# Converting the weights of the second MLP's first five chunks beside the first MLP, by way of HBM

## The chip, the cores and the metric

The kernel runs on one core of one Trainium2 chip. The metric is the device time of one execution in microseconds (us); the times of several runs are given by their median. The engines are TensorE (PE, with its weight loads as PEld), VectorE (DVE), ScalarE (ACT), GpSimd (POOL) and SyncE (SP), which here issues every transfer.

## What is computed

Three stages follow one another. A memory attention gives x, 2304 tokens by 512. The first MLP (d_ff 2048) and the second, bilinear one (d_ff 1536) follow:

```
a = softmax(phi, over the sequence);  k_m = a^T k;  v_m = a^T v
x = softmax(q k_m^T / 8) v_m                  # 4 batches, 8 heads, 576 tokens
h = x @ w_in;  g = max(0.01 h, h);  y = g @ w_out
out = ((y @ w_a) * (y @ w_b)) @ w_out2
```

All weights reach the kernel as 64-bit floating point numbers, seen as pairs of 32-bit words.

## The kernel before

**Weights.** Every weight tile (512 KB, 128 partitions x 512 numbers) is loaded by one transfer and converted on the chip by `weight()`. ACT takes the high and the low word apart (lines 441, 444), then come a clamp (448, DVE or POOL), a shift (452, DVE), a join (456, DVE) and an addition (459, DVE or POOL), which leave a 32-bit number. That number is split into two parts of the matmul's type: a high part (a copy, line 366 on ACT or 368 on DVE) and a low part (a subtraction, 465 for w_in and w_out, 957 for the matrices of the second MLP; DVE or POOL). Each product of two matrices takes three passes: high by high, high by low, low by high.

**First MLP.** It runs over four chunks of 512 hidden columns and, in each, over eight blocks of 288 tokens: four h units (line 759) and four y units (789) per block. The first layer is not applied to x: `vw` first multiplies v_m by the chunk's w_in (line 710), and h is that by the attention weights. The y parts are added up over the chunks in the tiles acc (DVE, line 801; the first chunk by a copy).

**Second MLP.** It runs in two sweeps over halves of the tokens, and in each over twelve chunks of 128 hidden columns. A chunk's two products are built from seven products (`ab_unit`, line 1001; tiles abx, aby, abz) of sums of the weight blocks (`w_sums`, line 940) with sums of the blocks of y (`y_blocks`, lines 836 and 866: tiles yt and yb). The tokens that are left over, 64 of each batch, go through in the first sweep directly (`y_left`, `left_unit`, 1044). The output product (`o_unit`, 1070) comes every second chunk, and its results are added up on DVE (1083). In the first sweep a chunk loads wa, wb and w_out2, converts and sums them, and `keep_weights` stores the five finished tiles (four wo, one w_out2) in HBM; in the second sweep `w_back` reads them from there.

**Order.** The program first lists all operations with the engines on which each can run, its estimated cost, the tokens that it reads and writes, and its tiles. A planner (`Program.order`) then plays the program through with these costs and writes down one order for each engine. PE's main units have written positions; every other operation has a due time that follows from the units that need it. An operation starts in the plan when its inputs are ready, its due time is no further off than `ahead`, and, if it opens a tile, more than `keep` rooms are free (24 "slot" rooms, and 20 "big" rooms that slots may use as well). Among those that are ready the one that is due first goes first. The plan lets only one of DVE and POOL work on SBUF operands of this kind at a time (`Port`). On the chip each engine then goes through its list in order and waits for its inputs; this holds for SP's transfers too.

Of the kernel before, what the change touches and what calls it, by code (L numbers as in the profile page):

```python
# [45 lines left out]
}  # L46


LEAD = 12
SLACK = {'win0': 5.57, 'wout0': 7.97, 'win': 4.58, 'wout': 5.1, 'wa': 2.19, 'wb': 5.78, 'wout2': 1.6, ('sc', 0, 0): 5.86, ('sc', 0, 1): 1.95, ('sc', 1, 0): 4.58, ('sc', 1, 1): -2.11, ('sc', 2, 0): 6.27, ('sc', 2, 1): 9.76, ('vw', 0, 0): 11.17, ('vw', 0, 1): 11.03, ('vw', 0, 2): 6.36, ('vw', 1, 0): -4.57, ('vw', 1, 1): 5.86, ('vw', 1, 2): 14.74}  # L50
START = 25.0
# [26 lines left out]
def c_dma(nbytes):  # L78
    return max(0.6, nbytes / 355e3)
# [239 lines left out]
def tile_mem_attention__leaky_mlp__bilinear_mlp(  # L319
# [37 lines left out]
    def two(n):  # L357

        return Port({"DVE": c_dve(n), "POOL": c_pool2(n)})

    def copy_by(n, psum=False):
        return (dict if psum else Port)({"ACT": c_act(n), "DVE": (c_dve(n) if psum else c_dve2(n)) + BIAS})
# [58 lines left out]
        "wout2": lambda c, k: w_out2[c * FC2:(c + 1) * FC2, :],  # L421
    }

    def weight(kind, c, k):
        key, raw, cv = (kind, c, k), ("raw", kind, c, k), ("cv", kind, c, k)
        tile_of(raw, "slot", [512], I64)
        if kind not in ("wa", "wb"):
            tile_of(key, "slot", [2, 512], F32R, heir_of=raw)
        tile_of(cv, "slot", [2, 512], I32)
        late = kind in ("wa", "wb", "wout2")  # L430
        first = kind in ("win", "wout") and c == 0

        def load(T):
            src = src_of[kind](c, k)
            nc.sync.dma_start(T[raw] if len(src.shape) == 2 else T[raw].rearrange("p (j f) -> p j f", j=src.shape[1]), src)

        def words(T, t, w):
            return T[raw].bitcast(t).rearrange("p (n t) -> p n t", t=2)[:, :, w]

        def high(T):  # L440
            nc.scalar.activation(T[cv][:, 0, :].bitcast(F32), words(T, F32, 1), AF.Abs)

        def low(T):
            nc.scalar.activation(T[cv][:, 1, :], words(T, U32, 0), AF.Copy, scale=2.0 ** -29)

        def clamp(T, e):
            a = T[cv][:, 0, :].bitcast(F32)
            engines[e].tensor_scalar(a, a, W_LEAST, W_MOST, op0=ALU.max, op1=ALU.min)

        def shift(T):  # L450
            a = T[cv][:, 0, :]
            nc.vector.tensor_scalar(a, a, 3, 0x3FFFFFF8, op0=ALU.logical_shift_left, op1=ALU.bitwise_and)

        def join(T):
            a = T[cv][:, 0, :]
            nc.vector.scalar_tensor_tensor(a, words(T, I32, 1), -0x40000000, a, op0=ALU.bitwise_and, op1=ALU.bitwise_or)  # L456

        def add(T, e):
            engines[e].tensor_tensor(T[cv][:, 0, :], T[cv][:, 0, :], T[cv][:, 1, :], op=ALU.add)

        def hi(T, e):
            copy(e, T[key][:, 0, :], T[cv][:, 0, :].bitcast(F32))

        def lo(T, e):
            engines[e].tensor_tensor(T[key][:, 1, :], T[cv][:, 0, :].bitcast(F32), T[key][:, 0, :].bitcast(F32), op=ALU.subtract)

        a = ("a", key)
        op("DMA", c_dma(524288), load, w=[raw], tiles=[raw], ahead=30.0, keep=2 if late else 7 if c < 2 else 4)
        op("ACT", 0.66, high, r=[raw], w=[a], tiles=[raw, cv], ahead=25.0, keep=0 if late else 5 if c < 2 else 2)
        op("ACT", 0.66, low, r=[raw], w=[("l", key)], tiles=[raw, cv])  # L470
        op(Port({"DVE": 0.42, "POOL": 2.0}), 0, clamp, w=[a], tiles=[cv])
        op(Port({"DVE": 0.42}), 0, shift, w=[a], tiles=[cv])
        op(Port({"DVE": 0.68}), 0, join, r=[raw], w=[a], tiles=[raw, cv])
        op(Port({"DVE": 0.62, "POOL": 1.35}), 0, add, r=[("l", key)], w=[a], tiles=[cv])
        if kind in ("wa", "wb"):
            return
        op(copy_by(512), 0, hi, r=[a], w=[("hi", key)], tiles=[cv, key])
        op(two(512), 0, lo, r=[a, ("hi", key)], w=[key], tiles=[cv, key], slack=SLACK[kind + "0" if first else kind])


    def kv_part(b, g):
# [431 lines left out]
            places[k] = hbm.tile([P, 2, 512], F32, name="k_" + "_".join(map(str, k)))  # L913
        return places[k]

    def w_sums(c):

        cvs = {"A1": ("cv", "wa", c, 0), "A2": ("cv", "wb", c, 0)}
        done = {"A1": ("a", ("wa", c, 0)), "A2": ("a", ("wb", c, 0))}
        ws = ("ws", c)  # L920
        tile_of(ws, "slot", [4, 256])

        def val(T, name):
            if name[0] == "S":
                return T[ws][:, int(name[1]) - 1, :]
            i = int(name[2]) - 1
            return T[cvs[name[:2]]][:, 0, i * 256:(i + 1) * 256].bitcast(F32)

        def tok(name):
            return (ws, name) if name[0] == "S" else done[name[:2]]  # L930

        def of(name):
            return ws if name[0] == "S" else cvs[name[:2]]

        for name, x, y, alu in (
            ("S1", "A21", "A22", ALU.add), ("S2", "S1", "A11", ALU.subtract), ("S3", "A11", "A21", ALU.subtract), ("S4", "A12", "S2", ALU.subtract)
        ):
            op(
                two(256), 0,
                lambda T, e, name=name, x=x, y=y, alu=alu: engines[e].tensor_tensor(val(T, name), val(T, x), val(T, y), op=alu),  # L940
                r=[tok(x), tok(y)], w=[tok(name)], tiles=[ws, of(x), of(y)],
            )
        for i, names in enumerate((("A11", "A12"), ("A21", "A22"), ("S1", "S2"), ("S3", "S4"))):
            k = ("wo", 0, c, i)
            if i < 2:
                tile_of(k, "slot", [2, 2, 256], F32R, heir_of=("raw", ("wa", "wb")[i], c, 0))
            else:
                tile_of(k, "slot", [2, 2, 256], F32R)
            wide = (
                (lambda T, i=i: T[cvs[f"A{i + 1}"]][:, 0, :].bitcast(F32).rearrange("p (x f) -> p x f", x=2))  # L950
                if i < 2 else (lambda T, i=i: T[ws][:, 2 * i - 4:2 * i - 2, :])
            )
            r = list(dict.fromkeys(tok(x) for x in names))
            op(copy_by(512), 0, lambda T, e, k=k, wide=wide: copy(e, T[k][:, :, 0, :], wide(T)), r=r, w=[(k, 0)], tiles=[k, of(names[0])])
            op(
                two(512), 0,
                lambda T, e, k=k, wide=wide: engines[e].tensor_tensor(  # L957
                    T[k][:, :, 1, :], wide(T), T[k][:, :, 0, :].bitcast(F32), op=ALU.subtract
                ),
                r=[*r, (k, 0)], w=[k], tiles=[k, of(names[0])], slack=5.0,  # L960
            )

    def keep_weights(c):
        for k in [("wo", 0, c, i) for i in range(4)] + [("wout2", c, 0)]:
            op(
                "DMA", c_dma(524288),
                lambda T, k=k: nc.sync.dma_start(kept(k).rearrange("p a b -> p (a b)"), flat(T[k])),
                r=[k], w=[("kept", k)], tiles=[k], ahead=1e12,
            )
# [2 lines left out]
        t = t.rearrange("p a b c -> p (a b c)") if len(t.shape) == 4 else t.rearrange("p a b -> p (a b)")  # L972
        return t.bitcast(F32)

    def w_back(c):
        for k in [("wo", 0, c, i) for i in (0, 2, 3, 1)] + [("wout2", c, 0)]:
            back = ("wo", 1, c, k[3]) if k[0] == "wo" else ("wout2", c, 1)
            tile_of(back, "slot", [2, 2, 256] if k[0] == "wo" else [2, 512], F32R)
            op(
                "DMA", c_dma(524288),  # L980
                lambda T, k=k, back=back: nc.sync.dma_start(flat(T[back]), kept(k).rearrange("p a b -> p (a b)")),
                r=[("kept", k)], w=[back], tiles=[back], ahead=30.0, keep=2,
            )
# [122 lines left out]
    for c in range(NC1):  # L1106
        for k in range(4):
            weight("win", c, k)
        for bs in ([0], [1], [2, 3]) if c == 0 else ([0, 1], [2, 3]):
            vw(c, bs)  # L1110
        for k in range(4):
            weight("wout", c, k)
        for n in range(NBLK):
            for f in range(4):
                h_unit(c, n, f, (step, (-6, -5, -3, -1)[f]))
            for e in range(4):
                y_unit(c, n, e, (step + 1, (-4, -2, 0, 1)[e]))
            step += 1
    y_blocks(0)
    y_left()  # L1120
    y_blocks(1)
    queue = []
    for s in range(2):
        if s:
            y_back(1)
        for c in range(NC2):
            if s:
                w_back(c)
            else:
                weight("wa", c, 0)  # L1130
                weight("wb", c, 0)
                w_sums(c)
                weight("wout2", c, 0)
                keep_weights(c)
# [50 lines left out]
```

## Time and profile before

| | |
|---|---|
| median of 3 runs | 837.1 us (835.94 to 838.3) |
| profiled execution | 838.8 us, span 836.7 us |
| PE busy | 799.5 us (96%) |
| DVE busy | 643.9 us (77%) |
| ACT busy | 360.2 us (43%) |
| POOL busy | 247.6 us (30%) |
| mean granted clock of PE | 0.988 |
| moved by DMA | 135.32 MB |

The span reaches from the first to the last instruction of the profiled execution; its time lies 2.1 us above its span. The busy shares are means over stages that differ: attention and the start of the first MLP to about 140 us, the first MLP to about 405, the first sweep of the second to about 640, the second sweep after that.

### The profile page before, as it was taken

What the parts mean: (1) busy time and instruction counts of PE and PEld (TensorE: products, weight loads), DVE (VectorE), ACT (ScalarE), POOL (GpSimd) and SP (SyncE); (2) the same over time, 40 slices, a digit from 0 to 9 for tenths busy, and PEclk for the clock granted to TensorE, in tenths of its full rate; (3) what the DMA queues carried; (4) which work ended last, traced back from release to release, by engine and by line L of the source; (5) the groups of instructions that cost most, each with busy time, mean ns of one, the idle gap of its engine ahead of it and who ended that gap; (6) DMA issues with size and microseconds to landing.
All of it is one profiled execution on the core that took longest, in us unless ns stands there. A gap on an engine that the chain in (4) does not pass through costs nothing.

```text
span 836.7 us, 13050 instructions
## 1 busy us (share of the span) xinstructions
PE 799.5 (96%) x4922; PEld 709.3 (85%) x4922; DVE 643.9 (77%) x1133; ACT 360.2 (43%) x788; POOL 247.6 (30%) x228
## 2 busy tenths in 40 slices
PE   5889999999999999988879999999999999999997
PEld 4578998999999999988768888888888888888886
DVE  6998898469846985799999999989965444565655
ACT  5665886556445645455446544534411121110100
POOL 4462376012201310166776334535520000000000
PEclk9999999999999999999989999999999999999999
DMA  9894300320121001014775777665578878545302
GB/s 327 315 286 144 127 2 0 111 92 1 51 82 71 1 1 51 27 52 178 256 259 212 273 283 268 225 243 191 187 271 320 310 229 271 202 151 176 125 1 101
DMA packets 50606, 135.32 MB, mean 162 GB/s; under 512 B 6384, under 2 KB 19696, under 8 KB 50544
## 3 DMA queue, kind: packets, MB, share of 16 engines
q1 hardware_dynamic: 50544, 134.50, 46.1%
q8 instruction: 38, 0.62, 0.3%
q14 instruction: 24, 0.20, 0.1%
HBM read 90.96 MB, written 43.52 MB: 161 GB/s over the span
## 4 chain that ended last, share of the span: by engine, by line
PE 75%; DVE 15%; DMA 4%; issue 4%; ACT 1%; POOL 1%; SPq 0%; DVEq 0%; ACTq 0%
PE y L789 20%; PE o L1070 15%; PE h L759 10%; PE aby L1001 9%; PE abx L1001 6%; PE abz L1001 6%; PE vw L710 2%; PE a L1044 2%; DVE t L1009 1%; PE b L1044 1%; DMA kvr<-in_kv_rest_dram 1%; DVE g L775 1%; DVE cv_wout L456 1%; PE sc L627 1%; DVE wo L957 1%
## 5 line engine op out<-in xcount | busy, mean ns | idle before, releaser
L789 PE MATMUL y<-g,wout 128*128 128x288 f32 x1536 | 224.5, 299 | 9.8 <-DVE acc L801 7.8
L789 PEld LDWEIGHTS y<-g,wout 128*128 128x128 f32 x1536 | 212.6, 191 | 14.5 <-DVE acc L801 9.4
L1070 PE MATMUL o<-p,wout 128*128 128x512 f32 x576 | 142.3, 391 | 1.5 <-DVE p L743 0.8
L1070 PEld LDWEIGHTS o<-p,wout 128*128 128x128 f32 x576 | 107.9, 188 | 25.8 <-DVE p L743 1.1
L1001 PE MATMUL aby<-yb_T,wo 128*128 128x512 f32 x432 | 112.3, 396 | 6.2 <-DVE t L1009 6.2
L1001 PEld LDWEIGHTS aby<-yb_T,wo 128*128 128x128 f32 x432 | 80.6, 189 | 23.9 <-DVE t L1009 7.5
L736 ACT ACTIVATE g<-h 128x288 fp32r<-128x288 f32 x128 | 52.6, 411 | 89.9 <-PE h L759 87.2
L1009 DVE TENSOR_TENSOR t<-aby,t 128x512 f32<-128x512 f32 x72 | 49.4, 686 | 52.6 <-PE aby L1001 50.2
L1083 DVE TENSOR_TENSOR oacc<-o,oacc 128x512 f32<-128x512 f32 x80 | 55.0, 688 | 37.9 <-PE o L1070 37.6
L759 PE MATMUL h<-ahi,vwh 128*128 128x288 f32 x256 | 77.3, 302 | 1.2 <-ACT ahi L366 1.2
L775 DVE TENSOR_TENSOR g<-t,g 128x288 fp32r<-128x288 f32 x100 | 57.9, 586 | 26.7 <-ACT t L736 26.6
L759 PE MATMUL h<-alo,vwh 128*128 128x288 f32 x256 | 76.7, 300 | 0.5 <-POOL alo L658 0.5
L759 PE MATMUL h<-ahi,vwl 128*128 128x288 f32 x256 | 76.2, 298 | 0.0
L366 ACT CAST p<-t 128x512 fp32r<-128x512 f32 x44 | 27.2, 621 | 109.7 <-DVE t L1022 83.5
L1001 PE MATMUL abx<-yb_B,wo 128*128 128x512 f32 x288 | 73.7, 391 | 0.0
L775 POOL TENSOR_TENSOR g<-t,g 128x288 fp32r<-128x288 f32 x28 | 24.5, 882 | 131.5 <-ACT t L736 101.2
L1001 PEld LDWEIGHTS abx<-yb_B,wo 128*128 128x128 f32 x288 | 53.6, 189 | 10.8
L801 DVE TENSOR_TENSOR acc<-y,acc 128x288 f32<-128x288 f32 x96 | 43.3, 451 | 24.5 <-PE y L789 23.7
L736 ACT ACTIVATE t<-h 128x288 f32<-128x288 f32 x128 | 52.2, 408 | 0.0
L759 PEld LDWEIGHTS h<-ahi,vwh 128*128 128x128 f32 x256 | 48.9, 191 | 2.7 <-ACT ahi L366 1.4
L759 PEld LDWEIGHTS h<-alo,vwh 128*128 128x128 f32 x256 | 49.1, 192 | 0.9 <-POOL alo L658 0.9
L759 PEld LDWEIGHTS h<-ahi,vwl 128*128 128x128 f32 x256 | 49.1, 192 | 0.0
(173 smaller groups left out, 1360.4 us busy)
## 6 DMA issues: line engine op xcount, KB each, us to landing
k_wo<-wo SPq DMA_DIRECT2D x48, 512.0 KB, 6.6
wo<-k_wo SPq DMA_DIRECT2D x48, 512.0 KB, 4.7
raw_wout<-in_w_out_dram SPq DMA_DIRECT2D x28, 512.0 KB, 5.2
raw_win<-in_w_in_dram SPq DMA_DIRECT2D x16, 512.0 KB, 4.8
kv<-in_kv_dram SPq DMA_DIRECT2D x16, 512.0 KB, 7.8
raw_wa<-in_w_a_dram SPq DMA_DIRECT2D x12, 512.0 KB, 3.8
raw_wb<-in_w_b_dram SPq DMA_DIRECT2D x12, 512.0 KB, 4.6
k_wout<-wout SPq DMA_DIRECT2D x12, 512.0 KB, 5.2
```

The costliest lines, as they stand in the source:

```text
L366: nc.scalar.copy(dst, src)
L710: nc.tensor.matmul(T[o][0:m], T[VM[v]][:, j, bs[0]:bs[0] + len(bs), :].rearrange("p b m -> p (b m)"), T[w][:, i, wcols], start=(k == 0), s ...
L736: nc.scalar.activation(dst, src, AF.Prelu, alpha=0.01)
L759: nc.tensor.matmul(T[o], T[w[u]][:, k, fs], T[a[v]][:, k, cols], start=(k == 0 and i == 0), stop=(k == 1 and i == 2))
L775: lambda T, e: engines[e].tensor_tensor(T[g][:, i, 1, :], T[t], T[g][:, i, 0, :].bitcast(F32), op=ALU.subtract),
L789: nc.tensor.matmul(T[o], w[:, u, es], g[:, v, :], start=(f == 0 and i == 0), stop=(f == 3 and i == 2))
L801: "DVE", c_dve(NB), lambda T: nc.vector.tensor_tensor(T[acc][:, e, :], T[o], T[acc][:, e, :], op=ALU.add),
L1001: nc.tensor.matmul(T[o], T[w][:, which, u, k * P:(k + 1) * P], T[ys[v]][:, k, :], start=first and k == 0 and x == 0, stop=k == 1 and x == ...
L1009: op("DVE", 0.69, lambda T: nc.vector.tensor_tensor(T[to], T[o], T[x], op=ALU.add), r=[o, x], w=[to], tiles=[o, x, to])
L1044: nc.tensor.matmul(T[o], T[w][:, k // 2, u, k % 2 * P:(k % 2 + 1) * P], T[ys[v]][:, k, :], start=(k == 0 and x == 0), stop=(k == 3 and x = ...
L1070: nc.tensor.matmul(T[o], T[w][:, u, es], T[g][:, at, v, :], start=(x == 0 and k == 0), stop=(x == 1 and k == 2))
L1083: "DVE", c_dve(size), lambda T: nc.vector.tensor_tensor(T[acc][:, i, :], T[o], T[acc][:, i, :], op=ALU.add),
```

## The change

With `PRE = 5`, the operations that load, convert, sum and store the weights of chunks 0 to 4 of the second MLP are listed ahead of the y blocks, under version -1. Their loads read a token: for chunk 0 that the second chunk's last w_out tile of the first MLP is converted, for the others that the first wo tile of the chunk before is stored. They have no due time that holds them back (`ahead` is 1e12), but a load needs more than eight free rooms and the first ACT step more than six. In the first sweep, chunks 0 to 4 then read their five tiles back with `w_back`, as the second sweep does for all chunks; the second sweep reads the same stored tiles. Chunks 5 to 11 stay as they were. No operation computes anything else than before.

```diff
+PRE = 5
-    def weight(kind, c, k):
+    def weight(kind, c, k, after=()):
+        early = k < 0
...
-        op("DMA", c_dma(524288), load, w=[raw], tiles=[raw], ahead=30.0, keep=2 if late else 7 if c < 2 else 4)
-        op("ACT", 0.66, high, r=[raw], w=[a], tiles=[raw, cv], ahead=25.0, keep=0 if late else 5 if c < 2 else 2)
+        any_time = 1e12 if early else 60.0
+        op("DMA", c_dma(524288), load, r=after, w=[raw], tiles=[raw], ahead=1e12 if early else 30.0, keep=8 if early else 2 if late else 7 if c < 2 else 4)
+        op("ACT", 0.66, high, r=[raw], w=[a], tiles=[raw, cv], ahead=1e12 if early else 25.0, keep=6 if early else 0 if late else 5 if c < 2 else 2)
...
-    def w_sums(c):
+    def w_sums(c, v=0):
...
-    def keep_weights(c):
+    def keep_weights(c, v=0):
...
-    def w_back(c):
-        for k in [("wo", 0, c, i) for i in (0, 2, 3, 1)] + [("wout2", c, 0)]:
-            back = ("wo", 1, c, k[3]) if k[0] == "wo" else ("wout2", c, 1)
+    def w_back(c, s):
+        v = -1 if c < PRE else 0
+        for k in [("wo", v, c, i) for i in (0, 2, 3, 1)] + [("wout2", c, v)]:
+            back = ("wo", s, c, k[3]) if k[0] == "wo" else ("wout2", c, s)
...
+    for c in range(PRE):
+        after = [("kept", ("wo", -1, c - 1, 0))] if c else [("wout", 1, 3)]
+        weight("wa", c, -1, after)
+        weight("wb", c, -1, after)
+        w_sums(c, -1)
+        weight("wout2", c, -1, after)
+        keep_weights(c, -1)
     y_blocks(0)
...
         for c in range(NC2):
-            if s:
-                w_back(c)
+            if s or c < PRE:
+                w_back(c, s)
             else:
                 weight("wa", c, 0)
                 weight("wb", c, 0)
```

The other changed lines hand `ahead=any_time` and the version to the same operations.

## Rows read from the trace of the kernel before

**Rows 1.** The page: busy time of each engine, and PE in 40 slices.
```profile
PE 799.5 (96%) x4922; PEld 709.3 (85%) x4922; DVE 643.9 (77%) x1133; ACT 360.2 (43%) x788; POOL 247.6 (30%) x228
...
PE   5889999999999999988879999999999999999997
```

**Rows 2.** Windows: length, each engine's busy us, granted clock, DMA share, GB/s.
```profile
60.00:140.00 80.00, 80.00 (x713) 73.85 (x712) 71.93 (x178) 56.15 (x152) 39.56 (x34) 1.00 0.25 78
140.00:355.00 215.00, 213.32 (x1557) 210.12 (x1556) 153.28 (x283) 117.33 (x272) 35.84 (x30) 1.00 0.15 47
355.00:460.00 105.00, 91.06 (x511) 80.97 (x510) 103.96 (x136) 55.94 (x106) 71.50 (x49) 0.93 0.54 191
460.00:620.00 160.00, 159.38 (x841) 136.71 (x841) 148.70 (x247) 67.45 (x124) 70.59 (x57) 1.00 0.67 244
```

**Rows 3.** Waits, 355 to 460 us: total, times, longest.
```profile
PE y L789 <- DVE acc L801: 7.8, 5, 2.3
```

**Rows 4.** PE's timeline: start, length, group, idle time before it.
```profile
355.66 3.34 PE L789 MATMUL y<-g,wout 128*128 128x288 f32 x24
...
402.99 4.97 PE L789 MATMUL y<-g,wout 128*128 128x288 f32 x24 [1.76 <-DVE acc L801]
...
419.29 1.95 PE L1001 MATMUL aby<-yb_T,wo 128*128 128x512 f32 x6 [2.80 <-DVE t L1009]
421.04 2.76 PE L1001 MATMUL abz<-yb_B,wo 128*128 128x512 f32 x6
...
426.51 1.52 PE L1001 MATMUL abz<-yb_T,wo 128*128 128x512 f32 x6
...
437.21 2.68 PE L1001 MATMUL aby<-yb_T,wo 128*128 128x512 f32 x6 [3.36 <-DVE t L1009]
439.68 2.12 PE L1001 MATMUL abz<-yb_B,wo 128*128 128x512 f32 x6
```

**Rows 5.** Lines, 355 to 460 us: conversion on DVE, then POOL.
```profile
L957 DVE TENSOR_TENSOR wo<-ws,wo 128x512 fp32r<-128x512 f32 x7 | 9.9, 1411 | 0.0
...
L940 DVE TENSOR_TENSOR ws<-cv_wa,cv_wb 128x256 f32<-128x256 f32 x1 | 0.4, 411 | 0.0
...
L957 POOL TENSOR_TENSOR wo<-cv_wb,wo 128x512 fp32r<-128x512 f32 x4 | 6.1, 1533 | 0.0
...
L940 POOL TENSOR_TENSOR ws<-ws,cv_wa 128x256 f32<-128x256 f32 x1 | 0.9, 948 | 0.0
```

**Rows 6.** Conversion lines one by one: duration min/median/max in ns.
```profile
L441 ACT ACTIVATE cv_wa<-raw_wa x12: 652/672/684, 354.1 to 581.9; 128x512 f32<-128x512 f32 x12
...
L448 DVE TENSOR_SCALAR cv_wb<-cv_wb x11: 410/412/1381, 360.0 to 567.1; 128x512 f32<-128x512 f32 x11
...
L456 DVE SCALAR_TENSOR_TENSOR cv_wa<-raw_wa,cv_wa x12: 674/678/693, 359.4 to 588.9; 128x512 int32<-128x512 int32 x12
...
L459 DVE CUSTOM_DVE_ANT_0 cv_wa<-cv_wa x11: 674/683/1643, 361.3 to 590.4; 128x1024 uint16<-128x1024 uint16 x11
...
L940 DVE TENSOR_TENSOR ws<-ws,cv_wa x7: 411/411/1021, 376.2 to 597.8; 128x256 f32<-128x256 f32 x7
...
L957 DVE TENSOR_TENSOR wo<-ws,wo x12: 673/680/2890, 379.2 to 604.2; 128x512 fp32r<-128x512 f32 x12
```

**Rows 7.** Timeline of PE and the chain of waits, around 140 us.
```profile
144.85 1.87 PE L789 MATMUL y<-g,wout 128*128 128x288 f32 x12 [1.47 <-ACT acc L366]
...
136.33 4.22 POOL cv_wout L459
```

**Rows 8.** DMA issues (KB each, median us to landing), and SP's timeline.
```profile
wo<-k_wo SPq DMA_DIRECT2D x48, 512.0 KB, 4.7
...
148.58 2.88 SPq L435 DMA_DIRECT2D raw_win<-in_w_in_dram  x4
...
324.42 0.38 SPq L435 DMA_DIRECT2D raw_wa<-in_w_a_dram  x1
```

**Rows 9.** Timeline of PE at the first vw product of the third chunk.
```profile
221.87 0.63 PE L710 MATMUL vw<-win,vm_hi 128*128 128x512 f32 x2
```

More of the change, by code (lines that the diff above doesn't have):

```diff
@@ L467, in weight @@
         a = ("a", key)
-        op("DMA", c_dma(524288), load, w=[raw], tiles=[raw], ahead=30.0, keep=2 if late else 7 if c < 2 else 4)
-        op("ACT", 0.66, high, r=[raw], w=[a], tiles=[raw, cv], ahead=25.0, keep=0 if late else 5 if c < 2 else 2)
[L470 to L474, printed above, removed]
+        any_time = 1e12 if early else 60.0
+        op("DMA", c_dma(524288), load, r=after, w=[raw], tiles=[raw], ahead=1e12 if early else 30.0, keep=8 if early else 2 if late else 7 if c < 2 else 4)
+        op("ACT", 0.66, high, r=[raw], w=[a], tiles=[raw, cv], ahead=1e12 if early else 25.0, keep=6 if early else 0 if late else 5 if c < 2 else 2)
+        op("ACT", 0.66, low, r=[raw], w=[("l", key)], tiles=[raw, cv], ahead=any_time)
+        op(Port({"DVE": 0.42, "POOL": 2.0}), 0, clamp, w=[a], tiles=[cv], ahead=any_time)
+        op(Port({"DVE": 0.42}), 0, shift, w=[a], tiles=[cv], ahead=any_time)
+        op(Port({"DVE": 0.68}), 0, join, r=[raw], w=[a], tiles=[raw, cv], ahead=any_time)
+        op(Port({"DVE": 0.62, "POOL": 1.35}), 0, add, r=[("l", key)], w=[a], tiles=[cv], ahead=any_time)
         if kind in ("wa", "wb"):
             return
-        op(copy_by(512), 0, hi, r=[a], w=[("hi", key)], tiles=[cv, key])
-        op(two(512), 0, lo, r=[a, ("hi", key)], w=[key], tiles=[cv, key], slack=SLACK[kind + "0" if first else kind])
+        op(copy_by(512), 0, hi, r=[a], w=[("hi", key)], tiles=[cv, key], ahead=any_time)
+        op(two(512), 0, lo, r=[a, ("hi", key)], w=[key], tiles=[cv, key], ahead=any_time, slack=SLACK[kind + "0" if first else kind])
     def kv_part(b, g):
@@ L914, in kept @@
         return places[k]
-    def w_sums(c):
-        cvs = {"A1": ("cv", "wa", c, 0), "A2": ("cv", "wb", c, 0)}
-        done = {"A1": ("a", ("wa", c, 0)), "A2": ("a", ("wb", c, 0))}
+    def w_sums(c, v=0):
+        any_time = 1e12 if v < 0 else 60.0
+        cvs = {"A1": ("cv", "wa", c, v), "A2": ("cv", "wb", c, v)}
+        done = {"A1": ("a", ("wa", c, v)), "A2": ("a", ("wb", c, v))}
         ws = ("ws", c)
@@ L940, in w_sums @@
                 lambda T, e, name=name, x=x, y=y, alu=alu: engines[e].tensor_tensor(val(T, name), val(T, x), val(T, y), op=alu),
-                r=[tok(x), tok(y)], w=[tok(name)], tiles=[ws, of(x), of(y)],
+                r=[tok(x), tok(y)], w=[tok(name)], tiles=[ws, of(x), of(y)], ahead=any_time,
             )
         for i, names in enumerate((("A11", "A12"), ("A21", "A22"), ("S1", "S2"), ("S3", "S4"))):
-            k = ("wo", 0, c, i)
+            k = ("wo", v, c, i)
             if i < 2:
-                tile_of(k, "slot", [2, 2, 256], F32R, heir_of=("raw", ("wa", "wb")[i], c, 0))
+                tile_of(k, "slot", [2, 2, 256], F32R, heir_of=("raw", ("wa", "wb")[i], c, v))
             else:
@@ L953, in w_sums @@
             r = list(dict.fromkeys(tok(x) for x in names))
-            op(copy_by(512), 0, lambda T, e, k=k, wide=wide: copy(e, T[k][:, :, 0, :], wide(T)), r=r, w=[(k, 0)], tiles=[k, of(names[0])])
+            op(copy_by(512), 0, lambda T, e, k=k, wide=wide: copy(e, T[k][:, :, 0, :], wide(T)), r=r, w=[(k, 0)], tiles=[k, of(names[0])], ahead=any_time)
             op(
@@ L959, in w_sums @@
                 ),
-                r=[*r, (k, 0)], w=[k], tiles=[k, of(names[0])], slack=5.0,
+                r=[*r, (k, 0)], w=[k], tiles=[k, of(names[0])], slack=5.0, ahead=any_time,
             )
-    def keep_weights(c):
-        for k in [("wo", 0, c, i) for i in range(4)] + [("wout2", c, 0)]:
+    def keep_weights(c, v=0):
+        for k in [("wo", v, c, i) for i in range(4)] + [("wout2", c, v)]:
             op(
```

## The prediction

> **What bounds the kernel now.** I read the page first: TensorE (PE) is busy for 799.5 of 836.7 us, so only about 37 us of its idle time exist to be won, and the 40 slices show where: at the start, at the very end, and in four slices in the middle [rows 1]. The start and the end are not touched by this change. The table by stretches then tells what limits the middle [rows 2]. From 140 to 355 us, the bulk of the first MLP, PE is busy for 213.32 of 215 us while VectorE (DVE) works 153.28 and POOL 35.84: PE bounds, and DVE has 61.7 us of room. From 355 to 460 us, the last half chunk of the first MLP and the first chunks of the second, DVE is busy for 103.96 of 105 us, POOL for 71.50, and PE loses 13.94 us. From 460 to 620 PE is again full (159.38 of 160) with DVE at 148.70. So the program has one place where DVE is the bound. The waits of that stretch confirm the direction: PE waits for acc additions and for the additions of the product sums, both DVE work in an in-order queue [rows 3, 4].
>
> PE loses there in a second way. Its granted clock is 0.93 over the stretch [rows 2], and in the timeline the groups right after an idle time are long: six 512-column passes take 1.52 us at 426.51, but 1.95, 2.76, 2.68 and 2.12 at 419.29, 421.04, 437.21 and 439.68; 24 y passes take 3.34 at 355.66 but 4.97 at 402.99 [rows 4]. The excess is 0.43 + 1.24 + 1.16 + 0.60 + 1.63 = 5.06 us. Some passes ran at the lower level (1.2 instead of 2.4 GHz) after PE had waited. The whole loss is 13.94 + 5.06 = 19.0 us; that is the ceiling, as nothing else that bounds is touched.
>
> **The change, part by part.**
>
> *Removed from the stretch.* Which DVE work fills it? Grouped by line, 21 rows of weight conversion (lines 368 on wo, 448 to 465, 940 and 957) sum to 66.6 of DVE's 104.0 us, and ten rows on POOL to 29.7 [rows 5]. By the counts (five wa, five wb, three or four w_out2) this is about 4.6 chunks, that is 14.5 us of DVE and 6.5 us of POOL each. These are the five chunks that the change converts earlier. Without them DVE has 37.4 us of work in 105, plus whatever part of the yb blocks it then takes from POOL: no longer the bound. I keep 2 us of the 19.0 as left over, since the last y groups have to share DVE with the sums over acc and the rest blocks in any case.
>
> *Moved into the first MLP.* Per chunk DVE has, at the medians, clamp 0.41, shift 0.41 (same kind of instruction as the clamp), join 0.68 and add 0.68 for three weights = 6.54; one low part of w_out2, like those of line 957, 0.68; four sums at 0.41 = 1.64; four low parts at 0.68 = 2.72: 11.6 us, and 58 us for five [rows 6]. That is the lower bound. The upper is what the crowded stretch shows, 14.5 x 5 = 72.5 us, as there POOL's instructions stretch DVE's. The room is 61.7 us from 140 to 355 [rows 2], plus what POOL (179 us free) takes, plus 355 to about 405, where the first MLP still runs. I take a value near the lower end, 60 to 65, because POOL was busy for only 17% in this stretch against 68% in the crowded one. So it fits, just. ACT gets 2 x 0.67 for each of three weights and five copies of about the same length, some 7.4 us a chunk and 37 in all, against 97.7 us free [rows 2, 6].
>
> What does a nearly full DVE cost PE in the first MLP? The trace has one stretch that is alike: from 60 to 140 us DVE works 71.93 of 80 us with POOL at 39.56, and PE loses nothing there [rows 2]; just behind it PE waits 1.47 us for an acc copy on ACT, and that stall is most of the 1.68 us lost from 140 to 355. The chain shows its cause: ACT's queue, in which that copy stands, had been held up by a w_out conversion of 4.22 us on POOL [rows 7]. Every early chunk puts five such copies, each behind a conversion, into ACT's queue, so this is the stall to expect. Lower bound nothing, then; upper, a loss at the rate of the crowded stretch, 19.0 / 105 x 215 = 39 us, where DVE is wholly full. The load that I expect (213 to 218 of 215, less what POOL takes) lies nearer the first. I take two more stalls of the size of that one, one for each of the two chunk changes still to come: 3.4 us.
>
> On the crowding there is a row and a rule. The conversions' slowest cases are far from the median: line 957 has 0.68 at the median and 2.89 at most, the clamp 0.41 and 1.38 [rows 6]. The Trainium skill (SBUF — State Buffer, section "Who interferes with whom") says that VectorE and GpSimd hold a shared port pair as an exclusive lock and that the later one is blocked for the whole instruction; the maxima agree with it. By that rule every conversion step that goes to POOL takes its full time from DVE's port work, and the sum would come out as in the third rival.
>
> *Added.* 25 reads of 512 KB in the first sweep, 13.1 MB, landing in 4.7 us at the median [rows 8]. In exchange 15 weight loads and 25 stores leave the crowded stretch, where the DMA share was 0.54 [rows 2]. Fewer bytes move there than before, so I cost the reads at nothing; their cover is the 30 us by which the planner issues them ahead. If that cover were gone, the first product would wait about one landing, 4.7 us.
>
> *SP's queue.* Each early chunk puts three loads and five stores into the one in-order queue. The stores wait for low-priority conversions, and the w_in and w_out loads of the next chunk stand behind them. Now these loads are issued as soon as a slot is free: four w_in loads at 148.58, although the vw products that use them run at about 222 [rows 8, 9]. That distance of 73 us is the cover, and it shrinks; I cost it at nothing in the main line and as a rival below.
>
> **Sum.** 19.0 - 2.0 - 3.4 = 13.6 us less. The profiled execution took 838.8 us (span 836.7), 1.7 us above the median of the runs, 837.1. So 825.2 against the profiled execution, and 823.5 against the median. The clean case lies between 816 (the whole ceiling, and a pair of microseconds from the first sweep) and 829.
>
> **The rivals.**
>
> 1. *Only part of it moves.* A load of an early weight needs more than eight free rooms, and the next chunk cannot start before the one ahead is stored. The first MLP holds 20 big tiles and most of the 24 slots. If only three of five chunks are ready by the end of the first MLP, two of them (29 of 66.6 us) stay where they were, the loss falls by 56% to about 8.4 us, and 837.1 - 10.6 + 3.4 = 830. For it: today no weight of the second MLP is loaded before 324 us, and that only because of its due time, so the trace cannot show the room. Against it: the last chunk frees slots throughout.
>
> 2. *The queue turns over.* The loads of w_in and w_out wait behind early stores, whose conversions get DVE only when nothing else is ready: at 28% of DVE's time free (61.7 of 215), 11.6 us of work take 40 us. If a load comes out 10 us ahead instead of 73, the conversion of four w_in tiles (four times 2.2 + 0.68 = 11.5 us of DVE) stands bare, some 12 us at each of two chunk changes: 837.1 - 17 + 24 = 844. It decides from 8.5 us of bare time per change; below that the kernel is still faster. Against it: the planner issues loads by due time, and in its plan a store is issued when its data are ready.
>
> 3. *DVE overfills in the first MLP.* With POOL taking 32.5 us of conversions, DVE's load is 153.3 + 72.5 = 225.8 in 215 us; the 10.8 us come out as PE waits for acc and g: 837.1 - 19.0 + 2 + 10.8 = 831. That a POOL instruction holds DVE up is seen in the maxima [rows 6]; against it is the stretch from 60 to 140.
>
> **How the numbers follow.** Chances: the clean case 0.45, part of it moves 0.20, DVE overfills 0.18, the queue turns over 0.17. The predicted time is that of the first, 823.5. From the clean case downward there is little below 816; the first and third rival lie at 830 and 831 with some spread, so a range of 814 to 840 leaves out the queue case and little more. A measurement of this kernel can tell about 0.3%, 2.5 us, from no change. Faster than that are nearly the whole clean case, 0.9 of rival 1 and 0.8 of rival 3: 0.44 + 0.18 + 0.14 = 0.76. Within it the rest of these, 0.06; slower 0.18, almost all from rival 2.
>
> **What would show it.** Right: conversion groups of wa, wb and w_out2 between 140 and 355 us on DVE; DVE under 85% from 355 to 460 with PE idle below 5 us and its clock back at 1.00; the first ab product after the last y with no gap. Rival 1: converted chunks still in that stretch. Rival 2: SP waiting for wo before a w_in load, and PE idle ahead of vw. Rival 3: PE waiting for acc between 140 and 355. The prediction is wrong if PE idle grows in the first MLP by more than 8 us, or if the 19 us in the transition stay although DVE is no longer full.

## The result, and the profile after

The changed kernel takes 827.6 us (median; 825.7 to 828.3) against 836.8 for the kernel before in the same runs: ratio 0.988, 95% interval [0.986, 0.991], 9.2 us less. The forecast was 823.5 in a range of 814 to 840. Direction came out as forecast, and so did the mechanism of the gain; the gain fell about 4 us short. That net hides two larger errors that partly cancel, a gain that was bigger than thought and a loss that was too, and the experiments pull them apart.

The page after, total busy time and the 40 slices. Line numbers have moved by 1 to 6: y is now line 793, acc 805, the seven products 1007, the conversion 444 to 468.

```profile
PE 793.3 (96%) x4922; PEld 704.4 (85%) x4922; DVE 633.0 (77%) x1141; ACT 359.0 (43%) x784; POOL 232.3 (28%) x224
...
PE   5889999999999999989899999999999999999997
```

Against [rows 1] two lossy slices are left in the middle where there were four. PE's busy time has itself fallen, by 6.2 us, with the same 4922 passes: in the middle fewer of them run at the lower clock. The windows after, in the stretches of [rows 2] and two shorter ones (columns as there), say where:

```profile
60.00:140.00 80.00, 80.00 (x712) 73.86 (x712) 71.21 (x176) 55.47 (x151) 39.52 (x34) 1.00 0.29 91
140.00:355.00 215.00, 210.27 (x1517) 204.83 (x1516) 186.97 (x335) 136.07 (x305) 81.57 (x66) 1.00 0.34 121
355.00:460.00 105.00, 98.84 (x595) 89.64 (x594) 74.40 (x115) 41.08 (x82) 25.21 (x18) 0.98 0.65 226
460.00:620.00 160.00, 160.00 (x848) 138.12 (x847) 138.24 (x233) 62.98 (x113) 55.19 (x47) 1.00 0.61 218
...
180.00:220.00 40.00, 38.33 (x286) 37.87 (x285) 38.02 (x67) 24.65 (x57) 16.01 (x11) 1.00 0.35 125
...
340.00:380.00 40.00, 36.46 (x258) 35.63 (x256) 39.87 (x57) 20.81 (x45) 27.41 (x22) 0.96 0.39 134
```

From 140 to 355 us DVE has gone from 153.28 to 186.97 and POOL from 35.84 to 81.57: the conversions are there. PE's idle time has gone from 1.68 to 4.73 us, and PEld's busy time from 210.12 to 204.83. From 355 to 460, DVE has fallen from 103.96 to 74.40, and PE still idles for 6.16 us. The last row explains that mean: in its first part, and in the 15 us ahead of it, DVE is still full, 39.87 of 40 us. PE's timeline there (start, length, group, idle time before it):

```profile
360.28 1.75 PE L793 MATMUL y<-g,wout 128*128 128x288 f32 x12
364.10 2.85 PE L793 MATMUL y<-g,wout 128*128 128x288 f32 x12 [2.07 <-DVE acc L805]
366.75 0.44 PE L763 MATMUL h<-ahi,vwh 128*128 128x288 f32 x1
...
368.92 1.74 PE L793 MATMUL y<-g,wout 128*128 128x288 f32 x12
...
374.61 1.84 PE L793 MATMUL y<-g,wout 128*128 128x288 f32 x12 [0.78 <-DVE acc L805]
377.14 1.84 PE L793 MATMUL y<-g,wout 128*128 128x288 f32 x12 [0.69 <-DVE acc L805]
...
404.00 1.75 PE L793 MATMUL y<-g,wout 128*128 128x288 f32 x12
405.58 1.53 PE L1007 MATMUL aby<-yb_T,wo 128*128 128x512 f32 x6
...
409.82 1.66 PE L1007 MATMUL abx<-yb_B,wo 128*128 128x512 f32 x6 [1.35 <-ACT t L1018]
412.22 1.66 PE L1007 MATMUL aby<-yb_T,wo 128*128 128x512 f32 x6 [0.74 <-DVE t L1015]
```

It is the pattern of [rows 4] again, a wait of 2.07 us for acc, then passes that take 2.85 instead of 1.75 us. The granted clock is 0.50 once in this stretch, from 364.6 to 368.0; before, it was so four times, for some 3.4 us from 382.9, 403.4, 420.5 and 437.5. The stalls at the seven products, 2.80 and 3.36 before, are down to 1.35 and less. What DVE did at 360 us shows in its own timeline:

```profile
360.71 1.29 DVE L840 TENSOR_TENSOR yt_T<-acc,yt_T 128x576 f32<-128x576 f32 x1
361.92 1.75 DVE L459 SCALAR_TENSOR_TENSOR cv_wout_-1_4380<-raw_wout_-1_4292,cv_wout_-1_4380 128x512 int32<-128x512 int32 x1
363.60 0.45 DVE L805 TENSOR_TENSOR acc<-y,acc 128x288 f32<-128x288 f32 x1
```

The names with _-1 are tiles of the early conversion. A join of an early w_out2 stands between the sums of y and the addition on which PE waits. It takes 1.75 us here, 0.68 at the median before [rows 6]. SP's timeline shows how far the early work reaches, and what it did to the loads of w_in:

```profile
172.89 2.53 SPq L438 DMA_DIRECT2D raw_win<-in_w_in_dram  x4
...
386.01 0.32 SPq L972 DMA_DIRECT2D k_wout_-1_5044<-wout_-1_5013  x1
```

The four w_in loads that were issued at 148.58 [rows 8] now go out at 172.89, still 50 us ahead of the products that need them (223.29). At the next chunk change the last of the four leaves at 267.80, 40 us ahead (308.15). PE waits for none of them. The last early store leaves at 386.01, so all five chunks are done before the second MLP begins.

### The profile page after: what moved, and what is told of

It reads as the page before. It is cut to its first block, busy times and chain, and to the rows that moved or that the text cites. A ratio compares the mean times of both kernels' runs of the same rounds, so it can differ in the third digit from the quotient of the medians.

```text
span 826.6 us, 13115 instructions
## 1 busy us (share of the span) xinstructions
PE 793.3 (96%) x4922; PEld 704.4 (85%) x4922; DVE 633.0 (77%) x1141; ACT 359.0 (43%) x784; POOL 232.3 (28%) x224
## 4 chain that ended last, share of the span: by engine, by line
PE 76%; DVE 12%; DMA 6%; issue 3%; ACT 2%; POOL 1%; SPq 0%; DVEq 0%; ACTq 0%
PE o L1076 18%; PE y L793 15%; PE aby L1007 12%; PE h L763 8%; PE abx L1007 8%; PE abz L1007 8%; DMA k_yb_B<-yb_B 2%; PE b L1050 2%; PE a L1050 2%; PE vw L714 2%; DVE g L779 2%; DVE acc L805 2%; DMA raw_win<-in_w_in_dram 1%; DMA kvr<-in_kv_rest_dram 1%; DVE cv_win L459 1%
## 5 line engine op out<-in xcount | busy, mean ns | idle before, releaser
L793 PEld LDWEIGHTS y<-g,wout 128*128 128x128 f32 x1536 | 210.2, 189 | 14.5 <-DVE acc L805 9.5
L1007 PE MATMUL aby<-yb_T,wo 128*128 128x512 f32 x432 | 110.4, 391 | 1.3 <-DVE t L1015 1.3
L367 ACT CAST p<-t 128x512 fp32r<-128x512 f32 x48 | 29.8, 621 | 118.5 <-DVE t L1028 96.3
L779 DVE TENSOR_TENSOR g<-t,g 128x288 fp32r<-128x288 f32 x98 | 55.0, 566 | 11.0 <-ACT t L740 10.8
L729 DVE TENSOR_TENSOR vwl<-vw,vwh 64x512 fp32r<-64x512 f32 (+1 forms) x64 | 39.8, 622 | 5.5 <-ACT vwh L367 3.8
```

The costliest lines, as they stand in the source:

```text
L367: nc.scalar.copy(dst, src)
L729: nc.vector.tensor_tensor(T[lk][to, j // 2, cols], T[o][i * 64:(i + 1) * 64, :], T[hk][to, j // 2, cols].bitcast(F32), op=ALU.subtract)
L779: lambda T, e: engines[e].tensor_tensor(T[g][:, i, 1, :], T[t], T[g][:, i, 0, :].bitcast(F32), op=ALU.subtract),
L793: nc.tensor.matmul(T[o], w[:, u, es], g[:, v, :], start=(f == 0 and i == 0), stop=(f == 3 and i == 2))
L1007: nc.tensor.matmul(T[o], T[w][:, which, u, k * P:(k + 1) * P], T[ys[v]][:, k, :], start=first and k == 0 and x == 0, stop=k == 1 and x == ...
```

## The experiments

Each kernel is compared with the kernel before in the same runs. Edits are against the changed kernel.

**1. The ceiling: early conversion left out, reads kept.**

```diff
+            k = ("wout", 1, 3) if c < PRE else k
...
-    for c in range(PRE):
-        after = [("kept", ("wo", -1, c - 1, 0))] if c else [("wout", 1, 3)]
...
+    op(
+        "DMA", c_dma(524288), lambda T: nc.sync.dma_start(kept(stand_in).rearrange("p a b -> p (a b)"), flat(T[stand_in])),
+        r=[stand_in], w=[("kept", stand_in)], tiles=[stand_in], ahead=1e12,
+    )
```

> This kernel leaves out the conversion of chunks 0 to 4 altogether: in both sweeps their five tiles are read from one stored tile of the first MLP that stands in for them, so the transfers of the sweeps stay and the early work is gone (the result is that of other weights). Theory (the gain is DVE time taken out of the transition, and its price is DVE time put into the first MLP): both at their best, 837 minus 15 to 19 = 818 to 822 us, the first vw product of the last chunk back within 1 us of the kernel before (303.9 us; 308.2 after the change), and PE idle from 140 to 355 us near 1.7 us instead of 4.7. Rival (the gain comes from a luckier order of the whole plan, not from the work moved): nothing special, 825 to 837.

Measured: 815.0 us, ratio 0.973 [0.971, 0.975]. Windows of this kernel:

```profile
140.00:355.00 215.00, 213.32 (x1556) 210.06 (x1555) 153.49 (x285) 115.54 (x269) 36.55 (x30) 1.00 0.13 45
340.00:380.00 40.00, 40.00 (x303) 40.00 (x302) 31.78 (x55) 16.86 (x41) 8.05 (x8) 1.00 0.26 96
355.00:460.00 105.00, 105.00 (x643) 95.79 (x642) 73.00 (x116) 39.48 (x80) 16.80 (x12) 1.00 0.63 224
```

PE has no idle time at all in the transition, with all 25 reads in place: they are hidden, as costed. (The early loads and all but one of the early stores are gone as well.) And 22.7 us (837.6 - 815.0) are to be had, not 19.0.

**2. The price alone: early conversion made, but the first sweep converts for itself as before.** For it to fit, the early w_out2 loads ask for three free rooms instead of eight, and the planner keeps the best order that it has when one of its rounds finds none.

```diff
-            if s or c < PRE:
+            if s:
...
-                keep_weights(c)
+                if c >= PRE:
+                    keep_weights(c)
```

> The early conversion is kept, with its stores, but its tiles are only read by the second sweep; the first sweep loads and converts chunks 0 to 4 itself, as the kernel before does (one room threshold of the early w_out2 load is 3 instead of 8, without which no order exists). So the price is paid and the relief is not given. Theory: 837 plus the 5.4 us that the first MLP lost = 842, 840 to 846, with the first vw of the last chunk 4 us later than before. Rival (the early work is free, the net loss of 3 us against the forecast is all in the transition): 837, within 2 us.

Measured: 854.2 us, 1.020 [1.018, 1.022], 17 us slower; a miss. The first MLP pays about what it pays in the changed kernel (table below), but the added work goes on costing later. Windows of this kernel:

```profile
355.00:460.00 105.00, 88.97 (x535) 80.67 (x534) 99.89 (x137) 54.39 (x108) 62.01 (x39) 0.93 0.42 147
460.00:620.00 160.00, 154.90 (x801) 132.87 (x800) 154.92 (x243) 76.51 (x139) 104.18 (x74) 0.98 0.54 192
```

DVE is full to 620 us, and PE idles there for 5.1 us where it idled for 0.6. So this kernel does not isolate the price in the first MLP: it loses time in three stretches.

**3. How many chunks.** `PRE = 3`, `PRE = 4` and `PRE = 8` in place of 5.

> Three chunks instead of five. Theory, everything in proportion: the first MLP loses 3/5 of 5.4 = 3.2 us, the transition gains 3/5 of 14 to 15 = 8.7 us, so 837 - 5.5 = 831 us. Rival (the transition only has to get below a full DVE, for which three chunks are enough): the whole gain at a lower price, 837 - 14 + 3 = 826 us or less.

> Four chunks instead of five; with three the time was 820.6 us, with five 827.6. Theory (the fifth chunk is what does not fit: from 360 to 380 us DVE is full with its conversion and the y blocks, and PE loses 3.5 us and its clock there, while a stretch below a full DVE loses nothing): four chunks finish before the y blocks, DVE stays below 95% from 360 to 380 us, 819 to 822 us. Rival (each chunk more costs the same): 824 us.

> Eight chunks instead of five. Theory (DVE has only 28 us left from 140 to 355 us after the change, and three more chunks need 35): they do not fit, the transition fills again, 828 to 834 us. Rival (the first MLP has more room, at 1.1 us a chunk, and the first sweep gets easier): 822 to 826 us.

Measured: three chunks 820.6 us, 0.979 [0.977, 0.982]; four 818.6, 0.979 [0.977, 0.981]; eight 831.5, 0.993 [0.991, 0.995]. Fewer chunks gain more. A gain in proportion to the chunks would have left three of them at 831, and that theory falls. Windows of four chunks, 340 to 380 and 355 to 460 us:

```profile
340.00:380.00 40.00, 40.00 (x303) 40.00 (x302) 35.20 (x58) 18.59 (x45) 11.04 (x10) 1.00 0.34 124
355.00:460.00 105.00, 105.00 (x648) 96.09 (x647) 80.72 (x131) 43.57 (x89) 19.21 (x14) 1.00 0.65 228
```

and of eight, the first of these:

```profile
340.00:380.00 40.00, 36.46 (x259) 35.76 (x258) 39.88 (x55) 21.33 (x47) 27.18 (x20) 0.96 0.41 141
```

With four chunks the early work all but ends in time (3.0 us of it are left on DVE in that stretch), DVE has 4.8 of 40 us free, and PE loses nothing at all. The fifth fills that stretch, and PE loses 3.5 us in it; eight do here what five do.

The mean over 40 us still hides something: the kernel before has only 34.40 us of DVE in this stretch, less than with four chunks, and PE loses 3.49 us. The second half of it tells them apart; before, five chunks and four chunks:

```profile
360.00:380.00 20.00, 16.51 (x122) 16.04 (x121) 20.00 (x24) 12.55 (x27) 16.00 (x11) 1.00 0.16 58
```

```profile
360.00:380.00 20.00, 16.46 (x110) 15.77 (x108) 20.00 (x25) 10.64 (x21) 14.31 (x11) 0.91 0.48 162
```

```profile
360.00:380.00 20.00, 20.00 (x152) 20.00 (x151) 17.74 (x26) 10.01 (x23) 6.84 (x6) 1.00 0.39 141
```

**4. Where the early work stands.** Three and two chunks, all of them behind the last w_out of the first MLP, which frees the first MLP and loads the 340 to 380 us stretch:

```diff
-PRE = 5
+PRE = 3
...
-        after = [("kept", ("wo", -1, c - 1, 0))] if c else [("wout", 1, 3)]
+        after = [("kept", ("wo", -1, c - 1, 0))] if c else [("wout", 3, 3)]
```

> Three chunks, but their loads wait for the last chunk's w_out of the first MLP, so that no early conversion lies beside the conversion of w_in and w_out for a next chunk (180 to 220 and 260 to 300 us, where DVE went from 87 to 95 and 97%). Theory (the 4.6 us that the first MLP loses with three chunks comes from these two full stretches): the first vw of the last chunk comes at 330 us as in the stand-in kernel (334.4 with three chunks), and unless the work then overfills the time from 300 to 400 us, 816 us; with overfilling 818 to 821. Rival (the loss comes with the early work wherever it lies): the 4 to 5 us come later, 820 to 823 us.

> Two chunks, begun after the last chunk's w_out of the first MLP. Theory (as before: first MLP free of loss; two chunks are 23 us of DVE, which has some 18 us free from 300 to 355 and more behind it; the transition keeps three chunks' work more than with five): 816 to 820 us. Rival (the transition needs the relief of three chunks at least): 823 us or more.

Measured: three 828.4 us, 0.990 [0.989, 0.992]; two 827.6, 0.989 [0.987, 0.991]. Both lie above the 816 to 821 us of their theories, in the second case as its rival said. The windows, three chunks and then two:

```profile
340.00:380.00 40.00, 35.56 (x260) 34.38 (x259) 39.89 (x55) 21.36 (x49) 25.87 (x18) 1.00 0.45 157
```

```profile
340.00:380.00 40.00, 35.10 (x259) 34.17 (x258) 39.03 (x56) 20.66 (x46) 21.31 (x16) 1.00 0.39 145
```

Two chunks in the wrong place leave the kernel where five that reach into it do: PE loses 4.4 and 4.9 us here, where DVE is full, though the chunks are fewer, and the free first MLP (table below) does not make up for it. (With three, PE also waits 4.5 us for a read of w_out2 at 436.40.)

**5. The reads.** In the changed kernel ACT stands for 8.99 us behind a store of a y block, with the copy for which PE waits at 409.82 behind it. ACT's timeline:

```profile
408.23 1.04 ACT L367 CAST yb_T<-yt_T 128x1024 fp32r<-128x1024 f32 x1 [8.99 <-DMA k_yb_B<-yb_B]
409.19 0.58 ACT L1018 COPY t<-abx 128x512 f32<-128x512 f32 x1
```

If the early reads crowd that store, issuing them later should help:

```diff
-                r=[("kept", k)], w=[back], tiles=[back], ahead=30.0, keep=2,
+                r=[("kept", k)], w=[back], tiles=[back], ahead=30.0 if s else 12.0, keep=2,
```

> Five chunks as in the change, but the tiles of the first sweep are read back at most 12 us ahead of their due time instead of 30. In the changed kernel ACT stands for 9.0 us at 399 us for a room that a store of yb holds, and PE loses 2.6 us behind it. Theory (rooms and transfer time taken by readbacks 30 us ahead cause that wait): the wait goes, 3 us less, 824 to 825 us. Rival (the stores are late because yb itself is late, from the full DVE before): no change, 826 to 829 us.

Measured: 828.9 us, 0.992 [0.989, 0.994], no gain. The wait on ACT changes its name (6.90 us for the sum yt_T on DVE, at 404.61), and PE loses more just before. PE's timeline:

```profile
402.94 3.19 PE L793 MATMUL y<-g,wout 128*128 128x288 f32 x12 [3.26 <-DVE acc L805]
405.97 1.56 PE L1007 MATMUL abx<-yb_B,wo 128*128 128x512 f32 x6
```

DVE is 39.94 of 40 us full from 340 to 380 in this kernel too. The time of the reads is not the cause.

**6. Another order of the same work.** To see whether the result hangs on one order of the planner: early loads ask for nine free rooms instead of eight, five chunks as before.

```diff
-keep=8 if early else 2 if late else 7 if c < 2 else 4)
+keep=9 if early else 2 if late else 7 if c < 2 else 4)
```

> Five chunks as in the change, with nine instead of eight free rooms asked for an early load: the same work in another order, made to see how much of 827.6 us is the order's accident. Theory (the fifth chunk does not fit ahead of the y blocks): DVE full from 340 to 380 us again, 825 to 830 us. Rival (accident): anywhere, 818 to 824 us among the likely times.

Measured: 826.7 us, 0.988 [0.986, 0.989]. This one other order leaves the time where it was.

**7. POOL beside DVE.** Four chunks, with the early clamp, addition, sums and low parts on DVE alone.

```diff
-        op(Port({"DVE": 0.42, "POOL": 2.0}), 0, clamp, w=[a], tiles=[cv], ahead=any_time)
+        op(Port({"DVE": 0.42, "POOL": 99.0 if early else 2.0}), 0, clamp, w=[a], tiles=[cv], ahead=any_time)
...
-                two(512), 0,
+                two(512, v < 0), 0,
```

> Four chunks, with the whole early conversion on DVE and none on POOL. Theory (the loss in the first MLP is DVE standing behind POOL's early instructions, 1.3 to 1.8 us each, some ten a chunk): DVE's own load grows by some 0.68 us for each of these but its waits go; the loss up to the last vw falls from 5 to 2 or 3 us, 815 to 817 us. Rival (DVE's time itself is what is short): DVE is fuller from 140 to 355 us than the 185 us with POOL's help, the loss grows, 820 us or more.

Measured: 820.2 us, 0.980 [0.979, 0.982], against 0.979 of the four chunks with POOL. From 140 to 355 us POOL falls from 75.28 to 48.00, and the loss in the first MLP from 5.5 to 4.3 us. From 140 to 460 POOL works 16.0 us less and DVE only 4.3 more, which suggests that DVE lost less to POOL than before; but part of the work came later, into the stretch from 340 to 380 (DVE 37.53 against 35.20), and the total is no better. Neither theory is confirmed: the loss fell by 1.2 of 5.5 us, in one execution of each kernel and not by more than the kernels with POOL's help differ among themselves (4.81 to 6.52, table below), and the total gained nothing.

**8. Staged.** The early chunks are spread: the first behind the last w_out of the second chunk of the first MLP, the next two behind that of the third, the fourth behind that of the last. Four chunks, then three:

```diff
-        after = [("kept", ("wo", -1, c - 1, 0))] if c else [("wout", 1, 3)]
+        after = ([("kept", ("wo", -1, c - 1, 0))] if c else []) + [("wout", (1, 2, 2, 3)[c], 3)]
```

> Four chunks, but each may only start after the conversion of a w_out of the first MLP: chunk 0 after that of its second chunk, 1 and 2 after the third, 3 after the last. So little of the early work lies beside the two conversions of w_in and w_out at 180 to 220 and 260 to 300 us. With four chunks unstaged the time was 818.6 us, and the first MLP lost about 5 us up to the last vw. Theory (that loss comes from these two full stretches, and four chunks still finish before the y blocks): loss under 2 us, 814 to 816 us. Rival (room is taken from the early work, which then ends beside the y blocks, as with three chunks begun at the last w_out): 820 to 828 us, with DVE full from 340 to 380.

> Three chunks, the first after the w_out of the first MLP's second chunk as in the change, the other two only after that of its third chunk. Theory (two prices: early work beside a full DVE at a chunk change, some 5 us unstaged and 2 us staged from the second chunk's second vw to the last chunk's; and work that reaches the stretch of the y blocks, nothing with three chunks): the three parts would be 166, 65 and 405 us, which is 2 to 3 us less than with four staged chunks or with three unstaged: 815 us, 813 to 817. Rival (staging pushes the third chunk into the y blocks, as it did when all three began at the last w_out): 819 us or more.

Measured: four 817.3 us, 0.976 [0.974, 0.978]; three **814.6 us, 0.9745 [0.972, 0.977]**, the fastest: a gain of 21.2 us on the kernel before in the same runs, where the kernel of experiment 1, which converts nothing early, gained 22.7. Four chunks fall between theory (814 to 816) and rival (820 and more): 4.5 us of early DVE work still lie between 340 and 380. Windows of three staged chunks:

```profile
180.00:220.00 40.00, 40.00 (x303) 40.00 (x302) 35.68 (x69) 25.31 (x59) 11.79 (x8) 1.00 0.29 105
260.00:300.00 40.00, 40.00 (x303) 39.97 (x302) 39.29 (x73) 26.20 (x60) 15.29 (x11) 1.00 0.48 168
140.00:355.00 215.00, 212.36 (x1542) 208.07 (x1542) 178.54 (x328) 132.52 (x299) 62.71 (x50) 1.00 0.28 96
340.00:380.00 40.00, 40.00 (x303) 40.00 (x303) 31.80 (x54) 16.57 (x40) 7.85 (x7) 1.00 0.26 93
355.00:460.00 105.00, 104.69 (x642) 95.21 (x641) 89.90 (x141) 48.89 (x98) 32.26 (x24) 1.00 0.70 246
```

From 180 to 220 us DVE is at 35.68 instead of 38.02 and PE loses nothing where it lost 1.67. From 340 to 380 there is no early conversion left. And two chunks that are still converted beside the y blocks fit: DVE 89.90 of 105, PE idle 0.31.

The runs side by side. "First MLP" is the time from the vw products of its second chunk to those of its last (in each the second group of them), by the start of these rows in PE's timeline (164.75 to 328.96, so 164.21 us before), as a difference; PEld is its busy time from 140 to 355 us, as a difference to 210.12; PE idle likewise, to 1.68. The last two columns are DVE's busy time and PE's idle time in the 20 us from 360 to 380. The time before is that beside the changed kernel; beside the others it lay between 835.8 and 837.6.

| kernel | time, us | first MLP | PEld 140 to 355 | PE idle 140 to 355 | DVE, 340 to 380 | DVE, 360 to 380 | PE idle, 360 to 380 |
|---|---|---|---|---|---|---|---|
| before | 836.8 | 0 | 0 | 0 | 34.40 | 20.00 | 3.49 |
| five chunks (the change) | 827.6 | +5.35 | -5.29 | +3.05 | 39.87 | 20.00 | 3.54 |
| 1: stand-in | 815.0 | +0.03 | -0.06 | 0.00 | 31.78 | 16.93 | 0.00 |
| 2: price alone | 854.2 | +6.72 | -8.64 | +5.99 | 37.10 | 20.00 | 2.39 |
| 3: three chunks | 820.6 | +4.81 | -4.80 | +2.91 | 33.32 | 17.79 | 0.00 |
| 3: four chunks | 818.6 | +5.51 | -5.60 | +3.35 | 35.20 | 17.74 | 0.00 |
| 3: eight chunks | 831.5 | +5.23 | -4.74 | +2.70 | 39.88 | 20.00 | 3.54 |
| 4: three, from the last w_out | 828.4 | +0.39 | -1.33 | +0.73 | 39.89 | 19.90 | 3.63 |
| 4: two, from the last w_out | 827.6 | +0.42 | -1.24 | +0.84 | 39.03 | 20.00 | 3.86 |
| 5: reads later | 828.9 | +5.86 | -5.37 | +3.32 | 39.94 | 20.00 | 4.83 |
| 6: five, another order | 826.7 | +6.52 | -6.50 | +4.83 | 38.52 | 19.14 | 2.85 |
| 7: four, DVE alone | 820.2 | +4.26 | -4.30 | +2.56 | 37.53 | 19.86 | 0.54 |
| 8: four, staged | 817.3 | +2.04 | -2.14 | +1.08 | 37.77 | 18.16 | 0.32 |
| 8: three, staged | 814.6 | +1.99 | -2.05 | +0.96 | 31.80 | 16.93 | 0.00 |

In the last two columns PE loses at most 0.32 us wherever DVE is busy for 18.16 of the 20 us or less, and between 0.54 and 4.83 above that.

## Why the prediction was right, and where it was off

**What bounds, and what is removed: right.** The transition was bound by DVE full of conversions. Without them, and with nothing put in their place, PE runs through it without a gap (experiment 1). The reads cost nothing, though the forecast that fewer bytes would move there is wrong: 226 GB/s from 355 to 460, and 191 before.

**The ceiling: 22.7 us instead of 19.0.** All of it lies in the transition. By the starts of the same PE work, the last chunk's vw comes at 328.96 before and at 329.72 in the stand-in, and a product of the first sweep, abx, at 469.04 and at 447.15: 22.65 us. The forecast summed PE's idle time and five groups that were long, and left out one that was as long, in the kernel before:

```profile
382.84 3.21 PE L789 MATMUL y<-g,wout 128*128 128x288 f32 x12 [2.27 <-DVE acc L801]
```

Twelve such passes take 1.75 us elsewhere, so this is 1.5 us of the 3.7. PE's idle time comes out low as well. The ends of passes are modelled in the trace: twelve y passes are listed with 1.75 us, but the next group starts 1.58 us after them (404.00 and 405.58), so the wait of 2.07 us at 364.10 is 2.24 from start to start (364.10 - 360.28 - 1.58), and a wait shorter than that difference would not show at all. The table has the effect in the first MLP: in the nine kernels that lose 2.0 to 6.5 us there, the path lengthens by 1.3 to 2.1 times the idle time that PE adds, while the fall in PEld's busy time matches it to 0.1 us in seven of them and to 0.5 in all. (In experiments 2 and 4 losses behind the last vw fall into the window as well.) The Trainium skill (Perfetto Trace Analysis, section "Identifying the Most-Contended Engine") says that matmul busy time is a poor measure of how close a kernel is to its limit, and that the busy share of the weight loads is a good one. The trace agrees in the first MLP: 5.29 us of PEld against 5.35 us of path, where PE's idle time says 3.05. In the transition, where passes of 288 and of 512 columns mix, the weight loads do not tell it either: 80.97 us before and 95.79 in the stand-in are 14.8 us apart, and the path says 22.65.

**The price in the first MLP: right place, another mechanism, 5.3 us instead of 3.4.** In idle time, the measure in which it was forecast, it is 3.05. But the stalls are not the two at chunk changes behind ACT's copies that were forecast. The waits of PE from 140 to 355 us (total, times, longest):

```profile
PE y L793 <- DVE acc L805: 2.7, 5, 1.0
PE y L793 <- ACT acc L367: 1.7, 2, 1.4
```

The waits for ACT are as before, 1.7 us in two. New are five waits for acc on DVE, at 203 to 229 and at 286 to 302 us, and these are what the third rival named. Its size, 10.8 us, was too large, as POOL took 45.7 us of the work and DVE grew by only 33.7. That the forecast of 3.4 lies so near to 3.05 is luck.

**The step that failed: "I keep 2 us of the 19.0 as left over", and with it "So it fits, just".** The room was summed over the first MLP and counted "355 to about 405, where the first MLP still runs", which is where the y blocks need DVE. The early work of the fifth chunk ended there: between 340 and 380 us early conversions still take 10.1 us of DVE (11 instructions) and 17.1 of POOL (13), added up over the early tiles (wa, wb, w_out2, ws, wo) in that stretch; in the kernels with three chunks that begin at the second chunk's w_out there are none. So the crowd was made shorter, not dissolved: DVE is full from 360 to 460 us before and from 340 to 380 after, and from 360 to 380 PE idles as long as before, 3.54 us and 3.49. What was left over shows in the starts of the same PE work, here in the changed kernel and then in the stand-in:

```profile
333.56 0.63 PE L714 MATMUL vw<-win,vm_hi 128*128 128x512 f32 x2
...
404.00 1.75 PE L793 MATMUL y<-g,wout 128*128 128x288 f32 x12
...
612.28 1.52 PE L1076 MATMUL o<-p,wout 128*128 128x512 f32 x6
...
812.68 10.28 PE L1076 MATMUL o<-p,wout 128*128 128x512 f32 x44 [0.75 <-DVE p L747]
```

```profile
329.72 0.63 PE L714 MATMUL vw<-win,vm_hi 128*128 128x512 f32 x2
...
394.40 1.75 PE L793 MATMUL y<-g,wout 128*128 128x288 f32 x12
...
599.88 1.52 PE L1077 MATMUL o<-p,wout 128*128 128x512 f32 x6
...
799.34 10.25 PE L1077 MATMUL o<-p,wout 128*128 128x512 f32 x44 [0.76 <-DVE p L747]
```

The changed kernel is behind by 3.84 us at the last chunk's vw, by 9.60 at the last y, by 12.40 late in the first sweep and by 13.34 at the last group of output products. The second and the third step, 5.8 and 2.8 us, are what was left over: 8.6 us in place of 2. Neither is there with four chunks, where PE is busy for 105.00 of 105 us (experiment 3). The last step, 0.9 us, falls into the second sweep, most of it in one wait for ACT (0.68 us, at 672.35). (The changed kernel came to the second chunk's vw 1.5 us sooner, ahead of all that the change touches, which is why the first step is 3.84 and not 5.3.) The sum with measured terms, 22.7 - 5.3 - 8.6 - 0.9 + 1.5 = 9.4, stands against 9.2 measured by the medians. That the forecast came as near as 4 us is in part luck: its ceiling was 3.7 us too low, which offsets almost half of the 8.5 us by which price and rest were.

**The signs.** Of those named, the conversions between 140 and 355, DVE under 85% in the transition (71%) and the first product right behind the last y (405.58) came. PE idle below 5 us (6.16) and a clock of 1.00 (0.98) did not.

**The rivals.** That only part moves: no, the last store of the five chunks leaves at 386 us. That the queue turns over: the loads did go out later, by 24 us at the first change, but 50 and 40 us of cover stayed. That DVE overfills in the first MLP: in part; the price it named is real but half as large, and the larger loss is at the end of the first MLP.

**Open.** Why a full DVE does not always cost: from 260 to 300 us the staged kernel has DVE at 39.29 of 40 and PE loses nothing, while the changed kernel loses 0.44 there at 38.87. What the queue holds just ahead of an acc addition may matter beside how full it is; that was not tried. Nor was it tried whether five chunks would fill DVE from 360 to 380 without POOL, which works 14.31 us there, and 6.84 with four chunks: experiment 7 took POOL away from four chunks only. And the 17 us of experiment 2 were located but not divided.

## What to carry to other kernels

Moved work paid here until the bound engine was just below full, and no further: three chunks, well placed, gave 21.2 of the 22.7 us that the stand-in showed to be had, and the fifth, in the unstaged kernels, took back 9 us. Measure the room by stretches as short as the crowd (20 us here, not 215), leave free the stretch in which the moved work would end beside the next peak, and release it in portions rather than as early as possible. Read a price on PE from the start of a fixed row. The weight loads gave the same in the first MLP, but not in the transition; PE's idle time gave it in neither.

## What the runs showed of the hardware that was not expected

That POOL's instructions stretch DVE's stands in the prediction, read from the maxima of [rows 6]; single pairs now show by how much. Beside a POOL subtraction that ran from 361.35 for 1.78 us, a join of 0.68 us took 1.75 at 361.92, and in the first MLP a DVE addition took 1.78 where 0.68 is its median before, beside another. The timeline of both engines there:

```profile
199.58 1.46 POOL L468 TENSOR_TENSOR win<-cv_win,win 128x512 fp32r<-128x512 f32 x1 [1.94 <-ACT win L367]
...
199.82 1.78 DVE L462 CUSTOM_DVE_ANT_0 cv_win<-cv_win 128x1024 uint16<-128x1024 uint16 x1
```

The addition ends 0.6 us after the subtraction, so it is as if it had waited for nearly all of it and then run its own length: 199.58 + 1.46 + 0.68 = 201.72, against 201.60 measured. For the join the same sum gives 361.35 + 1.78 + 0.68 = 363.81, against 363.67. Still, taking POOL out of the early work gained nothing in all (experiment 7).
